# The opening of a fused FNet and GEGLU kernel: another order on four engines

## The chip, the cores and the metric

The kernel runs on one core of a Trainium2 chip. Times are device microseconds of that core. The core has a matrix engine (TensorE, PE in the profile), a vector engine (VectorE, DVE), an activation engine (ScalarE, ACT), a general engine (GpSimd, POOL), a queue engine for transfers (SyncE, SP) and sixteen transfer engines. Each engine takes its own instructions in order. Where one engine needs what another makes, it waits on a semaphore.

## The reference

The input `x` has 8 blocks of 3008 rows and 256 columns. It is Fourier-transformed along its rows and along its columns, and the real part goes through a gated feed-forward block:

```python
X = np.fft.fft(x, axis=1)
X = np.fft.fft(X, axis=2)
y = X.real.reshape(24064, 256)
g = y @ w_gate                       # 256 x 1536
gelu = 0.5 * g * (1.0 + erf(g / sqrt(2)))
out = (gelu * (y @ w_val)) @ w_out   # 1536 x 256
```

## The kernel before

**The transform.** A row index is written as 94 groups of 32. The kernel folds each block first: rows and their mirror rows (the same rows counted from the end) are added, and columns are folded in the same way, which leaves an even and an odd half (`eo`, lines 221 to 229). The forward rows come with plain transfers; the mirror rows come with an indirect transfer (`gather`, line 163) over a small table of indices that POOL makes (`index_consts`, lines 270 to 273). Then a matrix G of sines and cosines is applied along the rows (`s1`, line 513, called stage 1 here). Its result is copied out of PSUM into the tile A (line 519 on ACT, line 521 on DVE). For block 0 the matrix II (identities, one of them negated) joins and transposes the pieces of A (`ch`, line 535; copies into Z at 541 and 543). The matrix TP of twiddle factors completes the rows (`tp_e`, lines 591 and 596; copies into the tiles E and O at 601 and 603). The transform along the columns isn't applied to the data; it is multiplied into the weights: `make_w` (lines 451 to 470) makes the weights for E, for O, and for O negated (`minus`: W_sb or w_minus, lines 466 to 470) from `w_raw` and the matrix CW.

**The feed-forward part.** Each block is cut into three chunks of at most 512 columns, and each chunk into 12 slices of the 1536. For a slice, `l1_gate` takes a PSUM tile `ps_g`, multiplies the even half E into it and adds the odd half O (line 674 for each matmul); ACT applies Gelu (line 690). `l1_value` does the same in a tile `ps_v`. `l1_gate2` and `l1_value2` reuse the two tiles for the mirrored columns, with the negated weights. The products land in `h_sb` (lines 713, 730, 738), and `l2_piece` (line 763) multiplies them with `w_out`. There are two PSUM buffers for `ps_g`, three for `ps_v`, two for `ps_dft` and one for `ps_o`; a tile that is taken when all buffers of its tag have been used takes the oldest of them, and its first write waits for that buffer's last reader.

**The order.** The program is written out by hand, with no scheduler: every engine gets its instructions in the order in which the Python code issues them. `opening()` brings block 0 to its first E and O; `feed()` then runs the 288 slices and threads the transforms of later blocks between them. What matters here is the order within `opening()`:

- SP issues the two transfers of the staged forward rows. POOL makes columns and rows of counting numbers (`pool_consts`, lines 276 to 279), the index table, and issues the first gather; then `pool_consts2` (lines 282 to 284) and the other transfers: a second gather, the remaining rows of block 0, the weights, block 1.
- DVE makes small columns from them (`vec_consts`, lines 316 to 321), fills constants (lines 296 to 313), and reduces the phases of G (`g_phases`, lines 331 to 346). Line 344 is the absolute value of the reduced phase, |d|; line 345 subtracts a quarter. ACT takes the sines of these for G (`g_rows`, line 351; `g_ends`, lines 357 and 361) and for CW (lines 366 to 376). DVE makes II (`identities`, lines 390 and 392) and finishes CW (`cw_rest`, lines 381 to 386).
- PE multiplies zeros meanwhile: 16 warm matmuls, and 8 more after the first two stage-1 groups (`warm`, line 832).
- DVE folds block 0 in five pieces: rows 9 to 12, 13 to 16, 5 to 8, 0, and 1 to 4. Each `fold_piece` is followed by its two stage-1 groups, `s1(0, jg, 0)` and `s1(0, jg, 1)`, for jg = 2, 1, 3, 0, called (jg, g) below. All copies of A but the last are on ACT.
- Between these lie the twiddle phases (`t_columns` line 397, `t_phases` lines 401 and 404, `t_reduced` lines 265 and 266, `t_sin` line 411, `t_write` line 415) and the load of the Gelu table (line 426).

Of the kernel before, what the change touches and what calls it, by code (L numbers as in the profile page):

```python
# [9 lines left out]
FP32 = mybir.dt.float32  # L10
BF16 = mybir.dt.bfloat16
AF = mybir.ActivationFunctionType
ALU = mybir.AluOpType
# [15 lines left out]
def kernel(  # L29
# [55 lines left out]
    def work(shape, dt, tag, bufs, name):  # L85
        return work_pool.tile(shape, dt, tag=tag, bufs=bufs, name=name)
# [167 lines left out]
    rr = work([128, 2 * NGP], FP32, "O", 2, "rr")  # L254
    rd = work([128, 2 * NGP + NK], FP32, "Z", 1, "rd")
    cf, cr, cd = (work([128, C], FP32, t, 4, f"small_{i}") for i, t in enumerate(("v", "v", "v")))
    tf, tr, td = (work([128, 128], FP32, t, 3, f"small_t{i}") for i, t in enumerate(("ve", "ve", "ve")))
    w_raw = work([128, 2, 2, F], BF16, "h", 2, "w_raw")

# [55 lines left out]
    def vec_consts():  # L315
        nc.vector.tensor_scalar(col_a, col_p, 0.5, -0.25, op0=ALU.mult, op1=ALU.add)
        nc.vector.tensor_scalar(col_a, col_a, MAGIC, -MAGIC, op0=ALU.add, op1=ALU.add)
        nc.vector.scalar_tensor_tensor(col_h, col_a, -2.0, col_p, op0=ALU.mult, op1=ALU.add)
        nc.vector.tensor_scalar(col_n0, col_p, 1.0 / C, None, op0=ALU.mult)
        nc.vector.tensor_scalar(sc_g[:, 1:2], col_h, -TWO_PI, None, op0=ALU.mult)  # L320
        nc.vector.tensor_scalar(sc_g[:, 0:1], col_h, TWO_PI, -TWO_PI, op0=ALU.mult, op1=ALU.add)

    def vec_consts2():
        nc.vector.tensor_scalar(col_e, col_h, -1.0, 1.0, op0=ALU.mult, op1=ALU.add)
        nc.vector.tensor_scalar(keep2, col_p, 1.0, -2.0, op0=ALU.min, op1=ALU.mult)


    def g_phases():
# [12 lines left out]
        d0, d1 = (_sub(rd, [[1, n]], o, part_num=NP) for o, n in ((2 * NGP, NK), (NGP, NGP)))  # L341
        nc.vector.scalar_tensor_tensor(d1, r[:, NK:], MAGIC, f[:, NK:], op0=ALU.subtract, op1=ALU.subtract)
        c = _sub(rd, [[1, NGP]], 0, part_num=NP)
        nc.vector.scalar_tensor_tensor(c, d1, -1.0, d1, op0=ALU.mult, op1=ALU.max)
        nc.vector.tensor_scalar(c, c, -0.25, None, op0=ALU.add)
        nc.vector.scalar_tensor_tensor(d0, r[:, 0:NK], MAGIC, f[:, 0:NK], op0=ALU.subtract, op1=ALU.subtract)

    def g_rows(j0, nj):

# [15 lines left out]
    def cw_phases():  # L365
        nc.scalar.activation(cf[:, 0:128], row_c, AF.Copy, scale=col_n0)
# [20 lines left out]

    def identities():

        nc.vector.tensor_scalar(  # L390
            _sub(II, [[128, 3], [1, 128]], 0), _sub(row_c, [[0, 3], [1, 128]], 0), col_p, None, op0=ALU.is_equal)
        nc.vector.tensor_scalar(II[:, 1, 1, :], row_c, col_p, -1.0, op0=ALU.is_equal, op1=ALU.mult)

    def t_columns():
        ps = psum("v")
# [274 lines left out]
    def ffn_work(b):  # L670
# [5 lines left out]
        def cols_of(ci, fc):  # L676
# [3 lines left out]
                cstate[ci] = {"h": h_tile(), "ps": {}, "pso": {}}  # L680
            return n, c0, E, O, cstate[ci], slice(fc * 128, (fc + 1) * 128)

        def l1_gate(ci, fc):
            def run():
                n, _, E, O, st, fs = cols_of(ci, fc)
                pg = psum("g")
                mm(pg, n, "g", "E", fs, E, True, False)
                mm(pg, n, "g", "O", fs, O, False, True)
                gl = gelu_tile()
                nc.scalar.activation(gl[:, 0, :n], pg[:, :n], AF.Gelu)  # L690
                st["ps"][fc] = [pg, gl]
            return run
# [12 lines left out]
        def l1_value(ci, fc):  # L705
            def run():
                n, c0, E, O, st, fs = cols_of(ci, fc)
                pv = psum("v")
                if three(ci, fc):
                    gl = st["ps"][fc][1]  # L710
                    mm(pv, n, "v", "E", fs, E, True, False)
# [4 lines left out]
                mm(pv, n, "v", "E", fs, E, True, True)  # L716
# [82 lines left out]
    def opening():  # L799
        stage[0] = stage_tile()  # L800
        xb[0] = xb_tile(0)
        for j0, nj, at in ((9, 8, 0), (0, 1, 8)):
            nc.sync.dma_start(
                out=_sub(stage[0], [[1, nj * C]], at * C),
                in_=ap_replace(x, ap=[[32 * C, NPX], [1, nj * C]], offset=x.offset + j0 * C))
        pool_consts()
        index_consts(0)
        cast_mirror(0, 9, 8)
        pool_consts2()
        cast_mirror(0, 5, 4)  # L810
        cast_forward(0, 1, 8)
# [23 lines left out]
            for f in fold_ops(0, j0, nj, nc.vector):  # L835
                f()

        vec_consts()
        vec_fills()
        warm(16)  # L840
        cw_phases()
        g_phases()
        columns = t_columns()
        g_rows(9, 7)
        cw_reduced()
        vec_fills2()
        vec_consts2()
        identities()
        cw_magnitude()
        cw_sin()  # L850
        cw_rest()
        g_ends()
        g_rows(1, 8)
        t_phases(columns)
        fold_piece(9, 4)
        first, second = fold_ops(0, 13, 4, nc.vector)
        first()
        t_reduced()
        second()
        s1(0, 2, 0)()  # L860
        s1(0, 2, 1)()
        t_sin()
        gelu_table()
        warm(8)
        fold_piece(5, 4)
        s1(0, 1, 0)()
        s1(0, 1, 1)()
        fold_piece(0, 1)
        s1(0, 3, 0)()
        s1(0, 3, 1)()  # L870
        fold_piece(1, 4)
        s1(0, 0, 0)()
        s1(0, 0, 1, "V")()
        minus = []
        make_w(0, 0, 256, m_at=minus, tag="o")()
        ch(0, 0, qs=(0,))()
        t_write()
        ch(0, 0, "V", qs=(1,))()
        ch(0, 1, qs=(0,))()
        ch(0, 1, "V", qs=(1,))()  # L880
        make_w(1, 0, 256, m_at=minus, m_engine="V", tag="g")()
        tp_e(0, 0, 0, "A", tag="v")()
        tp_e(0, 0, 1, "V", tag="v")()
# [155 lines left out]
```

## Time and profile before

| | us |
|---|---|
| median of 4 runs | 621.14 (619.97 to 621.4) |
| profiled execution | 621.0 |
| its span | 619.2 |
| PE busy in the span | 606.6 |
| VectorE busy | 576.5 |
| ScalarE busy | 425.3 |
| GpSimd busy | 508.8 |
| first gather issued / fold begins | 1.89 / 8.82 |
| first feed-forward matmul starts | 18.41 |

The span is the time between the first and the last instruction of one profiled execution. The profile lists busy times by engine, groups of instructions by source line, waits with what ended them, and the chain of work that ended last, which is followed backwards from the last instruction to whatever released it. A busy engine isn't the bound by itself; a wait counts where it lies on that chain. Starts are counted from the start of the span. An instruction's length runs from its start to its end, and on one engine the next can start some 0.1 us before that end.

### The profile page before, as it was taken

Reading aid. Unit: us, or ns where it says so; the run is one execution under the profiler, and the core shown is the slowest. Engines: PE = TensorE matmul, PEld = TensorE weight load, DVE = VectorE, ACT = ScalarE, POOL = GpSimd, SP = SyncE. Lnnn points to the kernel's source line nnn. Section 1 sums busy time; section 2 is a strip of 40 time slices with the busy share of each in tenths; the row PEclk is TensorE's granted clock in tenths of the full one; section 3 lists DMA queues with packets and bytes.
Section 4 is the critical chain, followed back from the end, with each engine's and each line's share of the span. In section 5 each row is a group of like instructions: output and inputs, shape, how many; then the busy total and the mean of one; then the engine's idle time right before and its main releaser. Section 6 shows DMA issues by size and latency. Waiting matters only on the chain.

```text
span 619.2 us, 12746 instructions
## 1 busy us (share of the span) xinstructions
PE 606.6 (98%) x4182; PEld 406.4 (66%) x4230; DVE 576.5 (93%) x940; ACT 425.3 (69%) x825; POOL 508.8 (82%) x513
## 2 busy tenths in 40 slices
PE   7999999999999999999999999999999999999997
PEld 4456666666666666666666666666666666666666
DVE  7789999999999999999999999999999999999992
ACT  6787677777766676666767677666776667666651
POOL 8979899999997999879997899969987555555561
PEclk8999999999999999999999999999999999999999
DMA  9951825546362354632653344543123322221123
GB/s 179 202 128 37 246 53 154 136 121 178 91 168 79 96 150 109 157 98 51 162 141 99 108 96 120 141 107 95 43 69 77 97 56 51 64 50 43 40 52 82
DMA packets 52466, 65.40 MB, mean 106 GB/s; under 512 B 7629, under 2 KB 47278, under 8 KB 50004
## 3 DMA queue, kind: packets, MB, share of 16 engines
q1 hardware_dynamic: 45472, 49.03, 30.3%
q0 software_dynamic: 6608, 15.29, 11.5%
q8 instruction: 33, 0.54, 0.4%
q10 hardware_dynamic: 320, 0.26, 0.2%
q14 instruction: 33, 0.27, 0.1%
HBM read 39.65 MB, written 30.17 MB: 113 GB/s over the span
## 4 chain that ended last, share of the span: by engine, by line
PE 93%; DMA 2%; issue 1%; SPq 1%; ACT 1%; DVE 1%; POOL 0%; DVEq 0%; POOLq 0%; ACTq 0%
PE ps_o L763 39%; PE ps_g L674 29%; PE ps_v L674 20%; PE ps_dft L555 2%; PE ps_dft L591 2%; DMA xb<-in_x_dram,idx 1%; SPq L668 1%; DMA out_dram<-out_sb 1%; PE ps_dft L451 1%; PE ps_o L832 0%; DMA O_sb<-yrow 0%; ACT A_sb L519 0%; PE ps_dft L535 0%; DVE h_sb L730 0%; ACT gelu_sb L690 0%
## 5 line engine op out<-in xcount | busy, mean ns | idle before, releaser
L738 POOL TENSOR_TENSOR h_sb<-gelu_sb,v_sb 128x512 bf16<-128x512 bf16 (+1 forms) x280 | 319.8, 1147 | 91.1 <-DVE v_sb L736 79.5
L763 PE MATMUL ps_o<-Wo_sb,h_sb 128*128 128x256 bf16 (+1 forms) x2232 | 334.5, 273 | 0.0
L763 PEld LDWEIGHTS <-h_sb 128*128 128x128 bf16 (+1 forms) x2304 | 228.7, 100 | 111.1 <-POOL h_sb L738 1.2
L690 ACT ACTIVATE gelu_sb<-ps_g 128x512 bf16<-128x512 f32 (+1 forms) x288 | 169.5, 589 | 99.5 <-PE ps_g L674 76.2
L718 DVE SCALAR_TENSOR_TENSOR ve_sb<-EB_sb,yw,ps_v 128x512 f32<-128x512 bf16 (+1 forms) x280 | 206.2, 737 | 20.8 <-PE ps_v L674 18.1
L674 PEld LDWEIGHTS <-W_sb 128*128 128x128 bf16 x1440 | 138.1, 98 | 81.6 <-issue 4.0
L734 DVE TENSOR_TENSOR h_sb<-gelu_sb,ps_v 128x512 bf16<-128x512 bf16 (+1 forms) x280 | 189.9, 678 | 1.4 <-ACT gelu_sb L699 1.0
L736 DVE SCALAR_TENSOR_TENSOR v_sb<-ve_sb,ps_v 128x512 f32<-128x512 f32 (+1 forms) x280 | 187.4, 669 | 0.0
L699 ACT ACTIVATE gelu_sb<-ps_g 128x512 bf16<-128x512 f32 (+1 forms) x288 | 168.8, 586 | 0.0
L674 PE MATMUL ps_g<-O_sb,W_sb 128*128 128x512 bf16 (+1 forms) x530 | 159.0, 374 | 2.8 <-DMA O_sb<-yrow 0.3
L674 PE MATMUL ps_g<-E_sb,W_sb 128*128 128x512 bf16 (+1 forms) x288 | 108.0, 375 | 0.7 <-ACT gelu_sb L699 0.3
L674 PE MATMUL ps_v<-E_sb,W_sb 128*128 128x512 bf16 (+1 forms) x287 | 107.6, 375 | 0.8 <-DVE W_sb L459 0.6
L674 PE MATMUL ps_v<-O_sb,W_sb 128*128 128x512 bf16 (+1 forms) x288 | 108.0, 375 | 0.1
L783 ACT ACTIVATE out_sb<-ps_o 128x512 f32<-128x512 f32 x92 | 55.0, 598 | 34.3 <-PE ps_o L763 34.1
L229 POOL TENSOR_TENSOR eo_sb<-ab_sb 94x512 bf16<-94x512 f32 (+1 forms) x70 | 77.7, 1112 | 0.4
L558 ACT ACTIVATE S_sb<-ps_dft 96x512 bf16<-96x512 f32 x56 | 33.0, 589 | 18.6 <-PE ps_dft L555 18.6
L225 POOL TENSOR_TENSOR ab_sb<-x_raw,x_raw 94x508 f32<-94x508 f32 (+1 forms) x30 | 33.0, 1100 | 0.0
L222 POOL TENSOR_TENSOR ab_sb<-x_raw,x_raw 94x508 f32<-94x508 f32 (+1 forms) x30 | 32.9, 1098 | 0.0
L555 PE MATMUL ps_dft<-eo_sb,G 94*96 94x256 bf16 x119 | 22.3, 272 | 0.0
L601 ACT ACTIVATE E_sb<-ps_dft 128x512 bf16<-128x512 f32 (+1 forms) x23 | 13.5, 588 | 8.9 <-PE ps_dft L591 8.9
L163 POOL DMA_INDIRECT x_raw<-in_x_dram,idx x18 | 17.2, 957 | 2.8 <-issue 0.6
L601 ACT ACTIVATE O_sb<-ps_dft 128x512 bf16<-128x512 f32 (+1 forms) x22 | 13.0, 589 | 7.6 <-PE ps_dft L591 7.0
(151 smaller groups left out, 206.2 us busy)
## 6 DMA issues: line engine op xcount, KB each, us to landing
out_dram<-out_sb SPq DMA_DIRECT2D x364, 64.0 KB
x_raw<-in_x_dram SPq DMA_DIRECT2D x10, 768.0 KB
Z_sb<-z SPq DMA_DIRECT2D x7, 768.0 KB
z<-S_sb SPq DMA_DIRECT2D x7, 576.0 KB
EB_sb<-yrow SPq DMA_DIRECT2D x6, 376.2 KB
z<-S_sb SPq DMA_DIRECT2D x7, 192.0 KB
x_raw<-in_x_dram SPq DMA_DIRECT2D x2, 640.0 KB
x_stage<-in_x_dram SPq DMA_DIRECT2D x1, 768.0 KB
```

The lines of the kernel that those rows point to most:

```text
L225: eng.tensor_tensor(ab(1, 1, up), mir(1, up), fwd(255, down), op=ALU.add)
L229: eng.tensor_tensor(_sub(eo, [[C, nj], [1, 128]], j0 * C + g * 128), ab(0, 0, [[1, 128]]), ab(1, 0, [[1, 128]]), op=op)
L555: nc.tensor.matmul(ps[:96, q * C : (q + 1) * C], G[:, j, :], _sub(eo, [[1, C]], j * C), start=(j == js[0]), stop=(j == js[-1]))
L674: nc.tensor.matmul(ps[:, :n], W[nm, part][:, fs], src, start=start, stop=stop, **kw)
L690: nc.scalar.activation(gl[:, 0, :n], pg[:, :n], AF.Gelu)
L699: nc.scalar.activation(_sub(gl, [[-1, n]], TOK + n - 1), pg[:, :n], AF.Gelu)
L718: nc.vector.scalar_tensor_tensor(ve[:, :n], EB_bufs[b][:, c0 : c0 + n], yw[:, fc : fc + 1], pv[:, :n], op0=ALU.mult, op1=ALU.add)
L734: nc.vector.tensor_tensor(st["h"][:, fc, 0, :n], gl[:, 0, :n], pv[:, :n], op=ALU.mult)
L736: nc.vector.scalar_tensor_tensor(_sub(vv, [[-1, n]], n - 1), ve[:, :n], 2.0, pv[:, :n], op0=ALU.mult, op1=ALU.subtract)
L738: nc.gpsimd.tensor_tensor(st["h"][:, fc, 1, :n], gl[:, 1, :n], vv[:, :n], op=ALU.mult)
L763: nc.tensor.matmul(pso[:m, half], st["h"][:, fc, sign, h0 : h0 + m], Wo_sb[:, fc, :], start=(fc == 0 and not (first and sign)), stop=(fc = ...
L783: nc.scalar.activation(_sub(osb, [[1, 2 * C]], 0, part_num=m), pso[:m, :], AF.Copy)
```

## The change

All of it is in the opening and in the first three feed-forward matmuls.

- POOL makes the index table and issues the first gather ahead of `pool_consts`.
- |d| and the identities move from DVE to ACT, the identities as Abs(column - row), then Relu(1 - that), then a negated copy. They use a new small tile, `apart`.
- `vec_consts` moves to the place where DVE would wait for |d|; its column `col_n0` stays early, in `vec_n0`. `cw_reduced` is issued before `g_rows`, and `t_phases` before `g_ends` and the second `g_rows`.
- `t_reduced` and `t_sin` come between the first two folds instead of inside the second.
- The eight warm matmuls become six, and one more is issued after (3, 1).
- The copy of (3, 1) into A goes from ACT to DVE. The copies of Z change engines: the first half of each pair on DVE, the second on ACT. `t_write` comes before all of `ch`.
- Before the first slice, the even halves of gate 0, value 0 and gate 1 are issued (`even_ahead`); `l1_gate` and `l1_value` take the tiles up from there. For the later slices nothing is changed.

```diff
@@ g_phases
-        nc.vector.scalar_tensor_tensor(c, d1, -1.0, d1, op0=ALU.mult, op1=ALU.max)
+        nc.scalar.activation(c, d1, AF.Abs)
+        nc.vector.scalar_tensor_tensor(d0, r[:, 0:NK], MAGIC, f[:, 0:NK], op0=ALU.subtract, op1=ALU.subtract)
+        vec_consts()
         nc.vector.tensor_scalar(c, c, -0.25, None, op0=ALU.add)
-        nc.vector.scalar_tensor_tensor(d0, r[:, 0:NK], MAGIC, f[:, 0:NK], op0=ALU.subtract, op1=ALU.subtract)
@@ identities
-        nc.vector.tensor_scalar(
-            _sub(II, [[128, 3], [1, 128]], 0), _sub(row_c, [[0, 3], [1, 128]], 0), col_p, None, op0=ALU.is_equal)
-        nc.vector.tensor_scalar(II[:, 1, 1, :], row_c, col_p, -1.0, op0=ALU.is_equal, op1=ALU.mult)
+        nc.scalar.activation(apart[:, 0:128], row_c, AF.Abs, scale=-1.0, bias=col_p)
+        nc.scalar.activation(
+            _sub(II, [[128, 3], [1, 128]], 0), _sub(apart, [[0, 3], [1, 128]], 0), AF.Relu, scale=-1.0, bias=1.0)
+        nc.scalar.activation(II[:, 1, 1, :], II[:, 0, 0, :], AF.Copy, scale=-1.0)
@@ ffn_work
+        ahead = {}
+
+        def even_ahead(nm, ci, fc):
+
+            n, _, E, _, _, fs = cols_of(ci, fc)
+            ps = ahead[nm, b, ci, fc] = psum(nm)
+            mm(ps, n, nm, "E", fs, E, True, False)
+
+        if b == 0:
+            even_ahead("g", 0, 0)
+            even_ahead("v", 0, 0)
+            even_ahead("g", 0, 1)
+
         def l1_gate(ci, fc):
...
-                pg = psum("g")
-                mm(pg, n, "g", "E", fs, E, True, False)
+                pg = ahead.pop(("g", b, ci, fc), None)
+                if pg is None:
+                    pg = psum("g")
+                    mm(pg, n, "g", "E", fs, E, True, False)
                 mm(pg, n, "g", "O", fs, O, False, True)
@@ opening
-        pool_consts()
         index_consts(0)
         cast_mirror(0, 9, 8)
+        pool_consts()
         pool_consts2()
...
-        vec_consts()
         vec_fills()
         warm(16)
+        vec_n0()
         cw_phases()
+        identities()
         g_phases()
         columns = t_columns()
+        cw_reduced()
         g_rows(9, 7)
-        cw_reduced()
         vec_fills2()
         vec_consts2()
-        identities()
         cw_magnitude()
         cw_sin()
         cw_rest()
+        t_phases(columns)
         g_ends()
         g_rows(1, 8)
-        t_phases(columns)
         fold_piece(9, 4)
-        first, second = fold_ops(0, 13, 4, nc.vector)
-        first()
         t_reduced()
-        second()
+        t_sin()
+        fold_piece(13, 4)
         s1(0, 2, 0)()
         s1(0, 2, 1)()
-        t_sin()
         gelu_table()
-        warm(8)
+        warm(6)
         fold_piece(5, 4)
         s1(0, 1, 0)()
         s1(0, 1, 1)()
         fold_piece(0, 1)
         s1(0, 3, 0)()
-        s1(0, 3, 1)()
+        s1(0, 3, 1, "V")()
+        warm(1)
         fold_piece(1, 4)
         s1(0, 0, 0)()
         s1(0, 0, 1, "V")()
         minus = []
         make_w(0, 0, 256, m_at=minus, tag="o")()
-        ch(0, 0, qs=(0,))()
         t_write()
-        ch(0, 0, "V", qs=(1,))()
-        ch(0, 1, qs=(0,))()
-        ch(0, 1, "V", qs=(1,))()
+        for pp in range(2):
+            ch(0, pp, "V", qs=(0,))()
+            ch(0, pp, qs=(1,))()
         make_w(1, 0, 256, m_at=minus, m_engine="V", tag="g")()
```

More of the change, by code (lines that the diff above doesn't have):

```diff
@@ L256 @@
     cf, cr, cd = (work([128, C], FP32, t, 4, f"small_{i}") for i, t in enumerate(("v", "v", "v")))
+    apart = work([128, C], FP32, "v", 4, "apart")
     tf, tr, td = (work([128, 128], FP32, t, 3, f"small_t{i}") for i, t in enumerate(("ve", "ve", "ve")))
@@ L318, in vec_consts @@
         nc.vector.scalar_tensor_tensor(col_h, col_a, -2.0, col_p, op0=ALU.mult, op1=ALU.add)
-        nc.vector.tensor_scalar(col_n0, col_p, 1.0 / C, None, op0=ALU.mult)
         nc.vector.tensor_scalar(sc_g[:, 1:2], col_h, -TWO_PI, None, op0=ALU.mult)
@@ L325, in vec_consts2, with vec_n0 @@
         nc.vector.tensor_scalar(keep2, col_p, 1.0, -2.0, op0=ALU.min, op1=ALU.mult)
+    def vec_n0():
+        nc.vector.tensor_scalar(col_n0, col_p, 1.0 / C, None, op0=ALU.mult)
     def g_phases():
@@ L707, in run @@
                 n, c0, E, O, st, fs = cols_of(ci, fc)
-                pv = psum("v")
+                pv = ahead.pop(("v", b, ci, fc), None)
+                if pv is None:
+                    pv = psum("v")
+                    mm(pv, n, "v", "E", fs, E, True, not three(ci, fc))
                 if three(ci, fc):
                     gl = st["ps"][fc][1]
-                    mm(pv, n, "v", "E", fs, E, True, False)
                     mm(pv, n, "v", "O", fs, O, False, True)
@@ L715, in run @@
                     return
-                mm(pv, n, "v", "E", fs, E, True, True)
                 ve = ve_tile()
```

## The prediction

> **What bounds the kernel now.** I read the whole-program views first. The chain of work that ended last gives its shares by engine:
>
> ```profile
> PE 93%; DMA 2%; issue 1%; SPq 1%; ACT 1%; DVE 1%; POOL 0%; DVEq 0%; POOLq 0%; ACTq 0%
> ```
>
> TensorE (PE) is the bound, and no line of its steady state is touched. The change can only move the moment at which the feed-forward matmuls start; what follows then shifts as one piece. So I followed the same chain through the opening, in order of time (start, length, what):
>
> ```profile
> 1.89 6.91 DMA xb<-in_x_dram,idx
> 8.80 0.02 issue
> 8.82 0.19 DVE eo_sb L221
> ...
> 10.59 2.73 PE ps_o L832 x8
> 13.32 0.33 PE ps_dft L513 x4
> 13.65 0.02 issue
> 13.68 2.03 ACT A_sb L519 x5
> 15.71 0.05 issue
> 15.76 0.39 PE ps_dft L535 x2
> ...
> 18.13 0.70 DVE O_sb L603
> ```
>
> The gather of the first mirror rows lands at 8.80, VectorE (DVE) folds, eight warm matmuls (L832) hold PE until 13.1, five copies of A on ScalarE (ACT) run one behind the other until 15.7, then the channel step (L535), the E and O copies and, at 18.87, the first gate's odd half. Next come the timelines of single engines, for what is beside the chain (start, length, engine, line; in brackets the idle time before):
>
> ```profile
> 5.80 1.04 ACT L351 ACTIVATE G<-rd,sc_g 94x336 bf16<-94x336 f32 x2 [2.06 <-DVE rd L345]
> 8.18 0.15 DVE L386 CAST CW<-col 128x1 bf16<-128x1 f32 x1
> 12.96 0.28 DVE L225 TENSOR_TENSOR eo_sb<-xb,x_stage 94x127 bf16<-94x127 bf16 x1
> 13.16 0.18 DVE L221 TENSOR_TENSOR eo_sb<-xb 94x8 bf16<-94x8 bf16 x1
> 14.16 0.57 PE L513 MATMUL ps_dft<-G,eo_sb 94*128 94x96 bf16 x5
> 15.11 0.56 DVE L521 CAST A_sb<-ps_v 128x384 bf16<-128x384 f32 x1 [1.11 <-PE ps_v L513]
> 18.73 0.48 DVE L470 TENSOR_SCALAR w_minus<-ps_g,keep 128x256 bf16<-128x256 f32 x1
> ```
>
> To be seen: DVE has finished its constants at 8.33, half a microsecond before the gather; it folds without a gap from 8.82 to 14.0, and then waits 1.11 for PE.
>
> **Gather first (POOL).** Four small instructions (L276 to L279, 0.84 to 1.37) go behind it, so it is issued near 1.37 instead of 1.89: 0.5 earlier. Does it land earlier? The DMA view of 2 to 5.4 us says what moved in that time (packets, MB, share of 16 engines):
>
> ```profile
> q1 hardware_dynamic: 161, 0.74, 80.6%
> q0 software_dynamic: 4, 0.02, 2.4%
> ```
>
> The staged forward rows (q1) hold the engines; the gather, issued 1.5 us before this ended, moved almost nothing. It waits for bandwidth. Gain between 0 and 0.5; I take 0, nearest to that row. POOL's total is unchanged, so the second gather stays at 3.9. What waits behind the gather's 1.13 of POOL time is late: row_k is ready at about 3.06 instead of 1.37, row_c still near 3.26.
>
> **G's constants.** The DVE chain of g_phases started at 2.64; it now waits for row_k and starts at about 3.11 (+0.47). L342 moves from 4.19 to 4.66 and ends at 5.23. |d| goes to ACT: 94x408 f32, nearest row L351 (94x384, 0.55 each), so 5.29 to 5.85; meanwhile DVE does L346 and vec_consts, five dependent small operations, 0.7 by their old rows, to 5.92. Then L345 (0.37) ends at 6.29: G's sines start at 6.32 instead of 5.80, +0.5. The identities add 0.40 + 0.55 + 0.29 on ACT (rows L366, L351, L372); they run from 3.6 to 4.8 in the 2.06 idle shown above: nothing on the path. If that cover were gone, they would cost 1.24. Here a rule speaks against the change: the Trainium skill, "ScalarE: Activation LUTs", Rules for kernel authors, sends relu and the like to VectorE, up to about three times faster per element in bf16. By the row, |d| on DVE took 0.58 for 408 f32 elements, so the move is even; by the rule it would be 0.19 against 0.55 and the move would cost 0.36 more. I take the row: the operands are f32.
>
> **When folding starts.** ACT's magnitude and two sines follow G's first rows, so cw_rest on DVE, which ended at 8.33, ends at about 8.33 + 0.52 = 8.85. DVE comes free just when the gather lands. Even a gather at 8.3 would gain nothing here, and the forward rows 1 to 8 of block 0 (cast_forward, issued 4.85, landed 6.9 later, 11.75) let fold_piece(5,4) start no earlier than the old 11.86. So the DVE folds keep their times: 0, at worst +0.1. t_reduced merely swaps with half a fold. Later on ACT, t_phases, the ends and G rows 1 to 8 finish at 10.7 (old 9.3), t_sin at 11.0, two A copies at 12.0, the Gelu table at 13.3 and its dump at 13.5 (old 13.25). That is still before it matters.
>
> **Warm matmuls.** 8 become 6 before (1,*), and one goes in later. Two at half clock are 0.43 each, so PE is free at about 12.25; the (1,0) matmuls, whose folds are ready at 12.4, start at 12.45 instead of 13.11. Then 0.33, 0.33, 0.40, 0.40 as before: (3,1) is issued at 13.57 and its result stands at 14.14.
>
> **The shared copy.** This is the step that decides. s1(0,3,1) is now copied by DVE, in program order ahead of fold_piece(1,4). DVE is free at 13.20 (old 13.16), waits for PE until 14.18, copies (0.47 to the next start) and folds only then: 14.65 to 15.49 instead of 13.16 to 14.0. Behind it wait the (0,*) matmuls: (0,0) at 15.20, (0,1) at 15.54, result 15.87, DVE copy 15.91 to 16.47. ACT has one copy less, but its last one now waits for the fold: 15.57 to 16.06. Before, both engines had finished A at 15.70. The channel step needs both, so its second matmul is at 16.5 and the step is about 0.65 late. Bounds: with PE at full clock (3,1) is done 0.4 earlier, giving +0.3; with a later fold start, +0.9. The halves of ch swap engines, with the same number of copies on each, 0.
>
> **Even halves ahead.** gE(0,0), vE(0,0), gE(0,1) now precede the first odd half. PE had two gaps there (0.46 from 18.41, less 0.22 work, and 0.05): room for two. But the third takes the second of two ps_g buffers, in which make_w's result still lies; its last reader is w_minus (L470), 18.73 to 19.21, on DVE behind the O copy. So gO(0,0) goes from 18.87 to 19.27 + 0.22 = 19.49; vO ends its slot at 19.92 instead of 19.52 (+0.40). gE(0,1), 0.22, is then done already: +0.2 net. Without that wait it would be -0.26.
>
> **Sum.** 0 (gather and folds) + 0.65 (A) + 0.2 (odd halves) = +0.85, rounded to +0.8. Against the profiled execution, span 619.2 and 621.0 with what lies around it, that gives 620.0 and 621.8. The median of the runs is 621.14, 0.14 above this execution, so 621.9. Downstream the chain waits only for PE, ACT and DVE work that shifts along (VectorE at 26, ACT at 33), so it is passed on whole.
>
> **Rivals.** *Faster:* the gather and the other loads come earlier, or (3,1) is done before DVE needs it. For it: DVE waited 0.49 for the gather, and ACT's five serial copies were on the chain. Its best: fold_piece(1,4) cannot start before its rows (issued 7.74, 5.3 to landing, 13.04), 0.12 earlier; DVE's last copy then ends at 15.0 instead of 15.70; with -0.26 from the even halves, -0.96: 620.2. Against it: (3,1) depends on the fold that ends at 13.24, so the round trip has to fit in nothing.
>
> *Slower, by the clock:* the wait on DVE leaves PE idle, and the clock falls. Two stretches (PE busy in the third column, clock behind POOL's):
>
> ```profile
> 8.00:11.40 3.40, 1.50 (x12) 0.77 (x13) 2.88 (x11) 3.02 (x9) 3.40 (x5) 0.96 1.09 191
> 11.40:14.80 3.40, 3.40 (x29) 2.29 (x28) 2.59 (x10) 2.92 (x6) 3.40 (x6) 0.53 1.31 176
> ```
>
> PE was busy for 1.50 of 3.40, with one pause of 2.1, and the clock was 0.53 in the next stretch. The skill's "TensorE: Matmul & The Clock Gate", Part 1, wants an idle window of about 3.4 us for that; by it, new pauses of 0.4 to 0.8 cost nothing. The row shows that a shorter pause was enough. In the changed kernel PE would be busy for about 2.6 of 3.4 between 11.4 and 14.8 (1.0 warm, 1.5 stage 1, 0.1 of the rest) and again between 14.8 and 18.2. If a stretch with less than some three quarters busy is punished, 3.4 us of matmuls run at half speed, up to 1.7, of which about 1.2 falls on PE's own chain: +2.0, 623.1. It decides from the point where PE's share in such a stretch drops under what the gate accepts, which lies between 1.50 and 3.04 of 3.40 by the rows.
>
> *Nothing:* ACT's saved copy and PE's early start cancel the DVE wait: within 0.3, 621.1.
>
> **How the numbers follow.** Main case 0.55 (own range +0.3 to +1.3, 621.4 to 622.4), faster 0.20 (620.2 to 621.0), clock 0.15 (622.4 to 623.8), nothing 0.10. A range from 620.4 to 623.0 leaves out about 2 in 10: the better half of the faster case and the worse half of the clock case. 0.2% is 1.24 us, about what a measurement of this kernel can tell from no change. Slower by more: the clock case, and a tenth from the main case's upper end, 0.25. Faster by more needs all bounds at once and something unseen: 0.09. The rest, 0.66, is within it.
>
> **What would show it.** Right: the gather issued near 1.4 and landing at 8.6 to 8.9; G's first sine near 6.3; a DVE idle of about 1 us before an A copy that stands ahead of the last fold; the first channel matmuls near 16.2 to 16.5; the third even half waiting for w_minus. Wrong: folds that start before 8.5, that copy without a wait, or a clock of 0.5 after 15.

## The result, and the profile after

| | before | after |
|---|---|---|
| median of the runs, us | 620.96 (54 runs, 619.5 to 622.85) | 621.96 (33 runs, 620.74 to 624.57) |
| ratio to before | 1 | 1.0018 [1.0011, 1.0025] |
| profiled execution / its span, us | 621.0 / 619.2 | 622.56 / 620.7 |

The changed kernel is about 1.1 us slower (0.0018 of 620.96; the interval gives 0.7 to 1.55). The chain of work that ended last has the same bound as before, TensorE:

```profile
PE 91%; DMA 1%; SPq 1%; issue 1%; DVE 1%; ACT 1%; POOL 0%; DVEq 0%; POOLq 0%; ACTq 0%
```

The timelines of single engines in the changed kernel (start, length, engine, line; in brackets the idle time before, and who ended it). First the constants:

```profile
1.66 1.11 POOL L163 DMA_INDIRECT xb<-in_x_dram,idx  x1 [0.62 <-POOL idx L272]
3.36 0.58 DVE L334 SCALAR_TENSOR_TENSOR ff<-row_j,row_k 94x408 f32<-94x408 f32 x1 [0.23 <-POOL row_k L280]
6.42 1.04 ACT L355 ACTIVATE G<-rd,sc_g 94x336 bf16<-94x336 f32 x2 [0.52 <-DVE rd L350]
8.80 0.16 DVE L390 CAST CW<-col 128x1 bf16<-128x1 f32 x1
8.88 0.19 DVE L221 TENSOR_TENSOR eo_sb<-x_stage,xb 94x8 bf16<-94x8 f32 x1
```

The phases of G wait for row_k, G's sines start at 6.42 (5.80 before), and DVE's last constant and its first fold follow each other without a gap at 8.88 (8.82 before). Then stage 1. First the kernel before, its last fold on DVE and its last copy of A on ACT:

```profile
13.58 0.42 DVE L225 TENSOR_TENSOR eo_sb<-xb 94x508 bf16<-94x508 bf16 x1
15.18 0.52 ACT L519 ACTIVATE A_sb<-ps_g 128x384 bf16<-128x384 f32 x1
```

The changed kernel, on DVE:

```profile
13.04 0.28 DVE L225 TENSOR_TENSOR eo_sb<-xb,x_stage 94x127 bf16<-94x127 bf16 x1
13.71 0.56 DVE L526 CAST A_sb<-ps_dft 128x384 bf16<-128x384 f32 x1 [0.39 <-PE ps_dft L518]
...
14.61 0.41 DVE L225 TENSOR_TENSOR eo_sb<-xb 94x508 bf16<-94x508 bf16 x1
15.46 0.56 DVE L526 CAST A_sb<-ps_v 128x384 bf16<-128x384 f32 x1 [0.44 <-PE ps_v L518]
```

DVE finishes a fold, waits 0.39 for the result of (3, 1), copies it, and only then begins the last fold, which ends at 15.02 (14.0 before). A is complete at 16.02 (15.70 before). Last, the first feed-forward matmuls: one line of before (PE, the odd half of gate 1), then the changed kernel on DVE and PE:

```profile
20.61 0.59 PE L674 MATMUL ps_g<-O_sb,W_sb 128*128 128x512 bf16 x2
```

```profile
19.63 0.69 DVE L608 CAST O_sb<-ps_v 128x512 bf16<-128x512 f32 x1 [1.76 <-PE ps_v L601]
20.24 0.47 DVE L475 TENSOR_SCALAR w_minus<-ps_g,keep 128x256 bf16<-128x256 f32 x1
20.77 0.39 PE L679 MATMUL ps_g<-E_sb,W_sb 128*128 128x512 bf16 x1 [0.54 <-DVE w_minus L475]
21.00 0.38 PE L679 MATMUL ps_g<-O_sb,W_sb 128*128 128x512 bf16 x1
22.30 0.59 PE L679 MATMUL ps_g<-O_sb,W_sb 128*128 128x512 bf16 x2
```

The third even half waits 0.54 for w_minus, with the first odd half behind it. The odd half of gate 1 starts at 22.30 (20.61 before).

So the two profiles differ by +1.69 at gate 1, in three pieces: A complete, +0.32; from there to the copy of O, 3.61 instead of 2.43, +1.18; from that copy to gate 1's odd half, 2.67 instead of 2.48, +0.19. In the middle piece only the copies of Z and `t_write` have moved. They don't explain it: without a half-clock stretch there, the piece takes 2.27 to 2.45 in the experiments below that have the new order (e1, e3, e7 to e11), and 2.43 in the kernels with the old one (before, e4, e6, e12). The stretches of the changed kernel explain it (window, its length, PE busy, PEld, DVE, ACT, POOL, granted PE clock, DMA share, GB/s):

```profile
7.40:11.40 4.00, 2.05 (x19) 1.34 (x19) 3.16 (x13) 3.87 (x15) 3.72 (x5) 1.00 1.04 187
11.40:15.50 4.10, 2.62 (x33) 1.49 (x32) 3.25 (x12) 3.44 (x8) 3.80 (x7) 0.99 1.32 185
15.50:19.10 3.60, 3.60 (x24) 2.65 (x21) 1.75 (x5) 1.85 (x5) 2.99 (x4) 0.53 1.21 192
```

Both profiled executions have one stretch at half clock. Before, it lay between 11.4 and 14.8, in stage 1; after, it lies in the channel step. In these two single executions it hides part of the edit's cost in stage 1 and puts another on the channel step. To tell edits from clock, each run's mean granted clock was used beside its time. A stretch of 3.5 us at 0.53 takes 1.65 us of 620 and so lowers the mean to about 0.997; more than one such stretch lowers it to 0.994 or less. The number of stretches in a run is worked out from its mean in this way; no profile shows more than one. In the table, every experiment stands beside the runs of before on its own chip:

| median us (number of runs) | all runs | clock 0.998 or more | 0.995 to 0.997 | 0.994 or less |
|---|---|---|---|---|
| after | 621.96 | 620.90 (3) | 621.62 (22) | 622.89 (10) |
| *before, with the next four* | 620.79 | 620.14 (18) | 620.98 (32) | 622.03 (1) |
| e1: copy on ACT | 621.02 | 620.90 (2) | 621.02 (10) | 621.90 (2) |
| e2: two halves ahead | 621.94 | 620.50 (2) | 621.93 (10) | 622.80 (2) |
| e3: more warm matmuls | 622.14 | 621.13 (6) | 622.21 (15) | 623.05 (1) |
| e4: front alone | 621.27 | 620.81 (5) | 621.35 (8) | |
| *before, with the next four* | 620.39 | 619.70 (19) | 620.58 (44) | 622.39 (2) |
| e5: copy alone | 621.99 | 620.62 (2) | 622.00 (12) | |
| e6: two halves alone | 620.00 | 619.50 (12) | 620.46 (10) | |
| e7: early warm matmuls | 621.66 | 621.55 (18) | 623.37 (2) | |
| e8: copy behind the fold | 619.74 | 619.70 (21) | 621.89 (1) | |
| *before, with the next four* | 620.53 | 620.16 (17) | 620.83 (31) | |
| e9: e8 with the old front | 619.75 | 619.75 (20) | | |
| e10: gather second | 621.62 | 620.75 (2) | 621.65 (11) | |
| e11: e8 without early warm | 620.16 | 619.54 (3) | 620.07 (6) | 621.25 (4) |
| e12: early warm alone | 620.88 | 620.88 (13) | | |

Runs of the kernel before with one stretch are 0.67 to 0.88 us slower than those with none (620.98 - 620.14, 620.58 - 619.70, 620.83 - 620.16). The runs of before that the result was measured against have no clock on record, so the changed kernel is set beside all three chips: inside the class of one stretch it is slower by 0.6 to 1.0. It has more than one stretch in 10 of 35 runs, against 3 of 164 of the kernel before, and none in 3 of 35, against 54 of 164.

A class says how many stretches a run had, not where. In the profiles the place matters: in the channel step a stretch costs 1.2 to 1.4 (3.61 in after and 3.83 in e5, for 2.43), in stage 1 about 0.5 (from the start of folding to A 6.88 in before, for 6.34 and 6.38 without a stretch in e6 and e12). Nor does a class hold everything else equal: how early the rows land may go with it, and no run here separates the two.

### The profile page after: what moved, and what is told of

The parts are those of the page before. It is cut to its first block, busy times and chain, and to the rows that moved or that the text cites. A ratio compares the mean times of both kernels' runs of the same rounds, so it can differ in the third digit from the quotient of the medians.

```text
span 620.7 us, 12746 instructions
## 1 busy us (share of the span) xinstructions
PE 606.8 (98%) x4181; PEld 406.3 (65%) x4229; DVE 576.0 (93%) x938; ACT 426.3 (69%) x828; POOL 508.0 (82%) x513
## 4 chain that ended last, share of the span: by engine, by line
PE 91%; DMA 1%; SPq 1%; issue 1%; DVE 1%; ACT 1%; POOL 0%; DVEq 0%; POOLq 0%; ACTq 0%
PE ps_o L784 38%; PE ps_g L679 29%; PE ps_v L679 19%; PE ps_dft L560 2%; PE ps_dft L596 2%; SPq L673 1%; DMA out_dram<-out_sb 1%; PE ps_dft L456 1%; DMA O_sb<-yrow 0%; ACT gelu_sb L710 0%; DVE h_sb L751 0%; PE ps_dft L540 0%; DVE v_sb L757 0%; DVE W_sb L464 0%; POOL h_sb L759 0%
```

## The experiments

The theory: the shared copy costs most, since it waits for PE ahead of the last fold, and the third even half adds 0.2. The rivals: the clock is what costs; the new front (gather, constants) costs; or the edits cost nothing and a stretch at half clock only moved. Each experiment's ratio is to the runs of before on its chip. Four readings of each profile recur: when folding starts, when A is complete, when the copy of O starts, and when gate 1's odd half starts.

| us | fold starts | last fold ends | A complete | O copy | gate 1's odd half | half clock |
|---|---|---|---|---|---|---|
| before | 8.82 | 14.00 | 15.70 | 18.13 | 20.61 | stage 1 |
| after | 8.88 | 15.02 | 16.02 | 19.63 | 22.30 | channel step |
| e1 | 8.88 | 14.05 | 15.76 | 18.14 | 20.81 | stage 1 |
| e2 | 8.87 | 15.18 | 16.34 | 19.68 | 22.01 | channel step |
| e3 | 8.87 | 16.03 | 17.02 | 19.30 | 21.97 | stage 1 |
| e4 | 8.88 | 14.38 | 15.75 | 18.18 | 20.65 | stage 1 |
| e5 | 8.25 | 14.44 | 15.44 | 19.27 | 21.75 | channel step |
| e6 | 8.27 | 13.43 | 14.61 | 17.04 | 19.31 | none |
| e7 | 8.88 | 14.91 | 15.91 | 18.33 | 21.00 | none |
| e8 | 8.88 | 13.97 | 14.96 | 17.25 | 19.53 | none |
| e9 | 8.26 | 13.41 | 14.41 | 16.69 | 18.96 | none |
| e10 | 8.99 | 15.82 | 16.82 | 19.27 | 21.94 | stage 1 |
| e11 | 8.88 | 13.97 | 14.97 | 17.24 | 19.52 | none |
| e12 | 8.71 | 13.90 | 15.09 | 17.52 | 20.00 | none |

**e1, the copy back on ACT.** From the changed kernel:

```diff
-        s1(0, 3, 1, "V")()
+        s1(0, 3, 1)()
```

> The changed kernel with one thing undone: the copy of (3,1) into A is on ScalarE again, so the last fold no longer waits for it. Theory that the copy ahead of the fold is the main cost: the last fold ends near 14.2 instead of 15.0, ScalarE's five copies end near 15.3, the first channel matmul comes 0.5 to 0.7 earlier at the same clock, and the time falls by 0.65 us, to 621.3 (0.1%). Theory that the clock alone is the cost: the fold is earlier, but matmuls after 15 us still run at half speed and the time stays within 0.2 us of the changed kernel's 621.96. Theory that nothing but chance separates the kernels: 621.0 to 622.0 with no order.

Measured: 621.02, ratio 1.0005 [0.9997, 1.0013]. The DVE timeline of this kernel:

```profile
13.63 0.42 DVE L225 TENSOR_TENSOR eo_sb<-xb 94x508 bf16<-94x508 bf16 x1
14.86 0.56 DVE L526 CAST A_sb<-ps_v 128x384 bf16<-128x384 f32 x1 [0.82 <-PE ps_v L518]
18.14 0.69 DVE L608 CAST O_sb<-ps_v 128x512 bf16<-128x512 f32 x1 [1.04 <-PE ps_v L601]
```

The last fold ends at 14.05 again, and the copy of O starts where it did before (18.14 and 18.13). One word takes most of the loss away. What is left, 0.20 at gate 1, is the even halves. But the profile of e1 also has its stretch in stage 1, so e1 and after differ in the clock as well: part of their distance at gate 1 is that. In time, with one stretch in both, e1 is 0.6 faster than after (621.02 to 621.62).

**e5, the copy alone.** From the kernel before, one word:

```diff
-        s1(0, 3, 1)()
+        s1(0, 3, 1, "V")()
```

> The kernel before with one thing of the change: the copy of (3,1) into A is on VectorE, ahead of the last fold. Theory: VectorE waits for it, the last fold ends 1.0 to 1.5 later (near 15.3), the first channel matmul comes 0.5 to 0.9 later than 15.76 and the time rises by 0.5 to 0.9 us. Rival, that the copy itself is free and only TensorE's clock after 15 us costs: the first channel matmul comes within 0.2 of 15.76 wherever the clock is full.

Measured: 621.99, ratio 1.0028 [1.0016, 1.0040]: 1.6 slower, more than was expected and more than the whole change costs. Its DVE timeline:

```profile
8.25 0.19 DVE L221 TENSOR_TENSOR eo_sb<-x_stage,xb 94x8 bf16<-94x8 f32 x1
13.14 0.56 DVE L521 CAST A_sb<-ps_dft 128x384 bf16<-128x384 f32 x1 [0.39 <-PE ps_dft L513]
14.03 0.41 DVE L225 TENSOR_TENSOR eo_sb<-xb 94x508 bf16<-94x508 bf16 x1
14.88 0.56 DVE L521 CAST A_sb<-ps_v 128x384 bf16<-128x384 f32 x1 [0.44 <-PE ps_v L513]
```

It is the picture of the changed kernel, the 0.39 wait included, 0.6 earlier since folding started 0.6 earlier. From the start of folding to A: 7.19. Without the copy and at full clock the same distance is 6.34 (e6) and 6.38 (e12); with it, 7.03 (e7), 7.14 (after), 7.19 (e5). So the copy costs A 0.65 to 0.85 at full clock, some 0.75. Ahead of the fold stand 0.39 of wait and 0.48 of copy; a little of that comes back because ACT has one copy less behind it. With the stretch in stage 1 it is 7.83 (e10) against 6.88 (before): +0.95. The rest of the 1.6 is not the copy's own length: the stretch of e5 lies in the channel step, which takes 3.83 instead of 2.43. At full clock e5 is 0.92 slower than before (two runs), with one stretch 1.42.

**e8, the same copy behind the fold.** From the changed kernel; with it go seven early warm matmuls (e7), one warm matmul less, and two halves ahead instead of three:

```diff
-            even_ahead("g", 0, 1)
...
         g_rows(1, 8)
+        warm(7)
         fold_piece(9, 4)
...
-        s1(0, 3, 1, "V")()
-        warm(1)
         fold_piece(1, 4)
+        s1(0, 3, 1, "V")()
         s1(0, 0, 0)()
```

> The changed kernel with three edits: the copy of (3,1) stays on VectorE but stands behind the last fold, only two even halves go ahead, and seven warm matmuls fill TensorE's longest pause (the single one after (3,1) is left out). Theory: the last fold ends near 14.1, A is complete near 15.1 instead of 15.7, the first odd half of gate 1 comes 0.6 to 0.9 earlier than in the kernel before, and the time falls by 0.5 to 0.9 us against it, to about 620.2. Rival, that the waits return later in the opening or behind slice 30: the odd half is earlier, the time is that of the kernel before within 0.2 us.

Measured: 619.74 (22 runs, 619.36 to 621.89), ratio 0.9990 [0.9982, 0.9997], faster than both kernels. Its DVE timeline:

```profile
13.55 0.42 DVE L225 TENSOR_TENSOR eo_sb<-xb 94x508 bf16<-94x508 bf16 x1
13.88 0.55 DVE L526 CAST A_sb<-ps_dft 128x384 bf16<-128x384 f32 x1
14.40 0.56 DVE L526 CAST A_sb<-ps_v 128x384 bf16<-128x384 f32 x1
17.25 0.69 DVE L608 CAST O_sb<-ps_v 128x512 bf16<-128x512 f32 x1 [1.04 <-PE ps_v L601]
```

No bracket stands behind the two A copies: PE's results are there when DVE comes. From the start of folding to A it is 6.08 here, 6.09 in e11 and 6.15 in e9, some 0.25 less than without the shared copy. In the opening, sharing the copies is worth something; its place ahead of the fold cost three times that. In time this doesn't show by itself: at full clock e8 and before are level (619.70 both), though gate 1 is 1.08 earlier in the profile. The lower median goes with the clock: 21 of 22 runs without a stretch, against 19 of 65 of before on that chip.

**e2, two halves ahead instead of three.** From the changed kernel:

```diff
-            even_ahead("g", 0, 1)
```

> The changed kernel with only two even halves ahead (gate 0 and value 0); gate 1's even half goes back to its old place. Theory that the third one waits for w_minus and holds up the odd halves: gate 0's odd half starts within 0.1 of the end of the O copy, the odd half of gate 1 comes 0.45 to 0.5 earlier against the O copy, and the time falls by 0.45 us, to 621.5. Rival, that the wait is hidden further on by VectorE: the odd half of gate 1 is earlier, but the span is the same.

Measured: 621.94, ratio 1.0013 [1.0005, 1.0021]. From the O copy to gate 1's odd half it is 2.33 instead of 2.67, 0.34 less, where 0.45 to 0.5 was expected. The time, expected to fall by 0.45, doesn't separate from that of the changed kernel.

**e6, two halves ahead alone.** From the kernel before: `even_ahead` with

```diff
+            even_ahead("g", 0, 0)
+            even_ahead("v", 0, 0)
```

> The kernel before with the even halves of gate 0 and value 0 ahead of the first odd half, and not that of gate 1. Theory: value 0's even half fills the wait for the O copy, the odd half of gate 1 comes 0.2 earlier than 20.61, and the time falls by 0 to 0.25 us; three ahead showed plus 0.2 at the same place. Rival, that the order of these halves changes nothing: within 0.05 of 20.61.

Measured: 620.00, ratio 0.9995 [0.9989, 1.0002]. In the columns of equal clock it stands 0.2 (619.50 to 619.70) and 0.1 (620.46 to 620.58) under before. The lines of its profile, DVE's first fold, ACT's last copy of A, DVE's copy of O, and gate 1's odd half on PE:

```profile
8.27 0.19 DVE L221 TENSOR_TENSOR eo_sb<-x_stage,xb 94x8 bf16<-94x8 f32 x1
14.15 0.46 ACT L519 ACTIVATE A_sb<-ps_g 128x384 bf16<-128x384 f32 x1
17.04 0.69 DVE L603 CAST O_sb<-ps_v 128x512 bf16<-128x512 f32 x1 [0.86 <-PE ps_v L596]
19.31 0.59 PE L674 MATMUL ps_g<-O_sb,W_sb 128*128 128x512 bf16 x2
```

Over all profiles the distance from the O copy to gate 1's odd half is 2.67 with three halves ahead (after, e1, e3, e7, e10), 2.47 to 2.48 with none (before, e4, e5, e12), and 2.27 to 2.33 with two (e2, e6, e8, e9, e11). The third half turns a gain of about 0.2 into a loss of 0.2.

**e4, the front alone.** The kernel before with the new order up to the first fold:

```diff
-        pool_consts()
         index_consts(0)
         cast_mirror(0, 9, 8)
+        pool_consts()
...
-        nc.vector.scalar_tensor_tensor(c, d1, -1.0, d1, op0=ALU.mult, op1=ALU.max)
+        nc.scalar.activation(c, d1, AF.Abs)
```

and with the identities, `vec_consts`, `cw_reduced` and `t_phases` where the changed kernel has them; `t_reduced` and `t_sin` stay where they were.

> The kernel before with only the front of the change: gather first, |d| and identities on ScalarE, vec_consts moved, cw_reduced and t_phases reordered. Everything from the first fold on is as before. Theory: the fold starts between 8.8 and 8.95 as before (8.82), and the time is that of the kernel before within 0.2 us. Rival, that the earlier gather is worth something: the fold starts near 8.4 and the time falls by 0.3 to 0.5. Rival, that the later constants of G cost something: the fold starts after 9.0, plus 0.2 to 0.5.

Measured: 621.27, ratio 1.0003 [0.9995, 1.0012]: not told from before. Folding starts at 8.88, and the fold of rows 5 to 8 waits 0.32 for its rows, as the one line of its DVE timeline shows:

```profile
12.31 0.19 DVE L221 TENSOR_TENSOR eo_sb<-xb 94x8 bf16<-94x8 bf16 x1 [0.32 <-DMA xb<-in_x_dram]
```

**e10, the gather second again.** From the changed kernel:

```diff
+        pool_consts()
         index_consts(0)
         cast_mirror(0, 9, 8)
-        pool_consts()
```

> The changed kernel with one thing undone: pool_consts comes ahead of the first gather again. Theory that the late row_k is what delays G's constants: g_phases starts near 2.2 to 2.6 instead of 3.36, cw_rest ends near 8.1 to 8.4 instead of 8.95, and the fold starts when the gather lands (8.2 to 8.9). The time falls by 0 to 0.4 us against the changed kernel. Rival, that |d| on ScalarE is what delays them: cw_rest still ends after 8.8 and nothing changes.

Measured: 621.62, ratio 1.0015 [1.0007, 1.0024]. DVE's timeline:

```profile
8.17 0.15 DVE L390 CAST CW<-col 128x1 bf16<-128x1 f32 x1
8.99 0.19 DVE L221 TENSOR_TENSOR eo_sb<-x_stage,xb 94x8 bf16<-94x8 f32 x1 [0.67 <-issue]
14.52 0.56 DVE L526 CAST A_sb<-ps_dft 128x384 bf16<-128x384 f32 x1 [1.20 <-PE ps_dft L518]
```

The constants are 0.63 earlier (8.17 for 8.80), so it was the late row_k that had held them. The fold still starts only at 8.99, after 0.67 of idle time. The profile names no releaser for it; the constants being done, the gathered rows are what is left to wait for. The last line is the case that the prediction drew: the stretch lies in stage 1, the wait is 1.20, and A is complete at 16.82.

**e3, eight and three warm matmuls instead of six and one.**

```diff
-        warm(6)
+        warm(8)
...
-        warm(1)
+        warm(3)
```

> The changed kernel with four more warm matmuls in the two pauses of TensorE: eight instead of six after the first two stage-1 groups, three instead of one after (3,1). Theory that these pauses let the clock fall: no stretch at half clock between 15 and 19 us in the profile, and the time falls by 0.5 to 0.9 us against the changed kernel. Rival, that the copy and the third even half are the whole loss: the time stays within 0.2 us, or rises by up to 0.4 where the added matmuls run at half clock and hold up stage 1.

Measured: 622.14, ratio 1.0020 [1.0013, 1.0027]. The clock fell all the same, while the warm matmuls ran (PE's timeline; the window's columns as above):

```profile
10.59 3.28 PE L853 MATMUL ps_o<-gelu_sb 128*128 128x512 bf16 x8
```

```profile
10.60:14.00 3.40, 3.40 (x18) 1.40 (x16) 2.69 (x10) 3.23 (x7) 3.40 (x6) 0.59 1.28 187
```

Eight warm matmuls at half clock hold PE until 13.87, and stage 1 behind them: A at 17.02. Over the runs they did one thing: more than one stretch is seen in 1 of 22, where the changed kernel has 10 of 35. It gained nothing in time. The other experiments point the same way. Without early warm matmuls, the kernels with six in this place have more than one stretch in 18 of 89 runs (after 10 of 35, e1 2 of 14, e2 2 of 14, e10 0 of 13, e11 4 of 13); those with eight have it in 4 of 235 (before 3 of 164, e3 1 of 22, and e4, e5 and e6 none of 49).

**e7, warm matmuls earlier.** From the changed kernel, seven more in PE's order ahead of the first stage-1 group, where PE paused:

```diff
         g_rows(1, 8)
+        warm(7)
         fold_piece(9, 4)
```

> The changed kernel with seven more warm matmuls in TensorE's longest pause, before the first stage-1 group (8.0 to 9.7). Theory that the clock is part of the loss: no stretch at half clock between 10 and 20 us; gate 1's odd half comes 0.5 to 0.7 later than the kernel before has it (20.61), instead of 1.7 later, and the time falls to about 621.5. Rival, that the half clock comes whatever is done there: it shows in 10 to 20 us again and the time stays near 622.

Measured: 621.66, ratio 1.0019 [1.0011, 1.0027]. A stretch of its profile, then DVE's timeline:

```profile
14.80:18.20 3.40, 3.34 (x36) 2.42 (x34) 1.90 (x6) 3.01 (x8) 2.63 (x4) 1.00 1.15 180
```

```profile
13.61 0.56 DVE L526 CAST A_sb<-ps_dft 128x384 bf16<-128x384 f32 x1 [0.39 <-PE ps_dft L518]
14.50 0.41 DVE L225 TENSOR_TENSOR eo_sb<-xb 94x508 bf16<-94x508 bf16 x1
```

The clock is full, the channel step takes 2.42 again, and the wait of 0.39 and the late fold are still there: they don't come from the clock. At gate 1 e7 is only 0.39 behind before, but its median is nearly as slow as that of after. Against before at equal clock it is 1.85 slower (621.55 to 619.70). Its opening accounts for 1.0 of that: gate 1 at 21.00, where e12, the kernel before with the same early warm matmuls, has 20.00. In its profile 1.0 more is lost between 143 and 176 us, where PE waits 0.7 for a late transfer (O_sb<-yrow).

**e12, the early warm matmuls alone**, in the kernel before (the same line).

> The kernel before with seven warm matmuls in TensorE's longest pause and nothing else. Theory: no stretch at half clock in 10 to 20 us, ScalarE's copies of A start 0.3 to 0.5 earlier against the fold, and the time falls by 0.3 to 0.6 us. Rival, that the half clock in stage 1 is hidden by ScalarE's copies: within 0.15 us of the kernel before. Rival, that the added matmuls hold up the first stage-1 group: plus 0.2 to 0.6.

Measured: 620.88, ratio 1.0005 [0.9997, 1.0013]. A fall of 0.3 to 0.6 was expected, and a rise of 0.35 came. All 13 runs have the full clock, and over e7, e8, e9 and e12 it is 72 of 75, where before has 54 of 164. So the early warm matmuls do keep the clock up. Yet at full clock e12 is 0.72 slower than before (620.88 to 620.16): what the clock gave is lost again, after the opening. The profile of e12 ends 0.19 behind before, though gate 1 was 0.61 ahead; between 143 and 226 us, where it falls back, its list of waits has on PE (source, then sum, number and longest):

```profile
PE ps_g L674 <- DMA O_sb<-yrow: 0.9, 1, 0.9
```

**e11, e8 without the early warm matmuls** (the line `warm(7)` taken out).

> The best version so far (copy of (3,1) behind the last fold, two even halves ahead) without the seven early warm matmuls. Theory that they hold the clock: in part of the executions a stretch of 3.4 us at half clock returns between 10 and 19 us, the executions spread more widely, and the median is 0.3 to 0.6 us above 619.74. Rival, that the order of the copies is the whole gain: the median is within 0.15 us of 619.74.

Measured: 620.16 (13 runs), ratio 0.9994 [0.9986, 1.0003]. Its profile goes through the opening as e8's does (gate 1 at 19.52 and 19.53), and then its lead of 1.08 over before is lost within 10 us, near 80 us (same list):

```profile
PE ps_dft L632 <- DMA Z_sb<-z: 1.0, 1, 1.0
```

Four of its 13 runs had more than one stretch at half clock; e8 had none such in 22. By the clock that favours e8; but at full clock e11 is 0.62 under before (three runs), where e8 is level, and the two intervals overlap.

**e9, e8 with the front of before**: gather second, |d| and identities on DVE, the constants, `t_reduced` and `t_sin` in their old order.

```diff
+        pool_consts()
         index_consts(0)
         cast_mirror(0, 9, 8)
-        pool_consts()
...
-        nc.scalar.activation(c, d1, AF.Abs)
+        nc.vector.scalar_tensor_tensor(c, d1, -1.0, d1, op0=ALU.mult, op1=ALU.max)
```

> The kernel before (gather, constants and identities in their old places) with the rest of the best version: seven warm matmuls before the first stage-1 group and six after it, the copy of (3,1) on VectorE behind the last fold, two even halves ahead, the new order of the channel step's copies. Theory that the new front makes the fold wait for constants instead of the gather: here the fold starts at 8.2 where the gather is early, or when it lands, and the time is 0.2 to 0.5 us below that of the same version with the new front (619.74). Rival, that later rows bind the folds anyway: the time is within 0.15 us of it.

Measured: 619.75 (20 runs, 619.15 to 620.35), ratio 0.9987 [0.9981, 0.9994]. From DVE's timeline:

```profile
8.26 0.19 DVE L221 TENSOR_TENSOR eo_sb<-x_stage,xb 94x8 bf16<-94x8 f32 x1
13.85 0.56 DVE L521 CAST A_sb<-ps_v 128x384 bf16<-128x384 f32 x1
```

Folding starts 0.62 before e8's, and gate 1's odd half is 0.57 earlier. The two medians are equal (619.75 and 619.74), but they come from two chips, on which before itself differs. Beside its own before at full clock e9 is 0.41 faster (619.75 to 620.16), and e8 is level; over all runs the ratios are 0.9987 and 0.9990, with intervals that overlap. So the new front may cost up to 0.6 by the profiles and 0.4 by the times, and these runs don't settle it. e8 and e9 both beat the kernel before.

## Why the prediction was right, and where it wasn't

The prediction was 621.9; 621.96 was measured, inside the range and in the class that it held likeliest. The main step was right, but the sum had errors that cancelled, a rival was partly true, and that the two figures lie 0.06 apart is luck. The prediction added 0.8 to 621.14, the median of four runs; over 54 runs before is 620.96, and the loss is 1.0 to 1.1.

- **Gather first.** Right that there is no gain. It was issued at 1.66, not 1.37, since the wait for the index table is 0.62 when nothing lies between; it took 6.9 and landed at 8.56. The transfers of 2 to 5.4 us fit the reason given (packets, MB, share of 16 engines): the forward rows moved nearly all of it, the gather next to nothing.

```profile
q1 hardware_dynamic: 189, 0.77, 83.5%
q0 software_dynamic: 9, 0.04, 8.4%
```

- **G's constants.** Right: sines at 6.42 for 6.32. |d| took 0.54 on ACT for 0.58 on DVE: the trace's row held, and the factor of about three that the Trainium skill ("ScalarE: Activation LUTs", Rules for kernel authors) gives to VectorE, stated there for bf16, did not carry over to these f32 operands.
- **When folding starts.** Right between the two profiles (8.88 for 8.82, predicted 8.85), but wrong as a bound. It took the 8.82 of one execution as the time at which the rows land. With the old front, e5, e6 and e9 fold from 8.25 to 8.27, and e6 starts rows 5 to 8 at 11.36, which the step held impossible before 11.86. Landing times scatter by 0.7 from profile to profile (8.16 to 8.86 with the new front); the old constants were ready at 8.33 and could use an early gather, the new ones, ready at 8.96, can't. "0, at worst +0.1" should have been 0 to +0.6 in a profile; in the times it is not settled (e9).
- **Warm matmuls and the shared copy.** Mechanism right: the wait, the late fold and the late A are in every profile that has the copy there, and go when it goes behind the fold (e8, e11). Size: +0.65 predicted; some +0.75 at full clock, +0.95 with the half-clock stretch in stage 1. The profile of after shows only +0.32 because it had the full clock in stage 1 and before had not: it compares two clocks. The lower bound of the step (+0.3, "with PE at full clock") made the same mistake: it sped PE up after the change, and left before at half clock.
- **Even halves ahead.** Right: +0.19 for +0.2, and for two halves -0.15 to -0.2, where -0.26 was said for the case without the wait. The wait for w_minus stands in the line.
- **The rival by the clock.** It was listed as another outcome; in fact it came beside the main one. In the profile the stretch moved to the channel step and cost 1.18 there, as the rival's 1.2 said, while the 0.5 that it had cost before in stage 1 went away. Over the runs, before has such a stretch in most of its executions too. What is new is that 10 of 35 have more than one, and only 3 have none. Those ten raise the median from 621.62, that of the 22 with one stretch, to 621.96: +0.3. The rival blamed the wait on DVE. The counts point elsewhere, to the warm matmuls that were taken out: 18 of 89 runs with six, 4 of 235 with eight. e5, which has the wait and all eight, has none of 14; e3, which differs from after in warm matmuls alone, has 1 of 22. The prediction counted their removal as a gain for PE only. This is a count and not a trace of those runs, e3 adds two further ones behind (3, 1), and e10 with six has none of 13: it is likely, not shown.
- **Sum.** Between the two profiles the 1.69 splits into fold start +0.06, copy at full clock +0.78 (7.14 for 6.36, the middle of e6 and e12), the stretch in the channel step instead of stage 1 +1.18 - 0.52, and odd halves +0.19. Over the runs it closes less exactly: copy and halves make +0.94 to +0.97 at full clock, where +0.8 was predicted from +0.65 and +0.2; measured are 0.6 to 1.0 with one stretch, and about 1.1 with the clock's share. Where the stretch lay in those runs is not known.
- **Passed on whole.** Nearly true between these two profiles: the first Gelu of slice 1 starts 1.70 later on ACT, the last Gelu of the program 1.55 later. It isn't a rule. In every profile the distance to before stays constant from slice 1 to about 70 us; then it shifts by up to 1.3 where a later block's rows or its Z come late (the lines of e11 and e12, and 0.3 in before itself near 93 us). Gains in the opening are partly given back there; e12, e11 and e7 show it.

## What to carry to other kernels

On an engine that works in order, a copy that waits for a round trip through another engine belongs behind the work that others wait for: in the opening, the same shared copy cost some 0.75 us ahead of the last fold, and saved 0.25 behind it. An early half of a product is worth issuing only into a buffer that is already free. And before two profiles are subtracted, set the clock of each stretch side by side: the same edit showed +0.32 or +0.95 according to where the half-clock stretch fell. Runs on different chips are compared through the kernel before on each.

## What the hardware showed that was not expected

- The clock fell after PE pauses much shorter than the stretch itself. The prediction had cited "TensorE: Matmul & The Clock Gate", Part 1, of the Trainium skill for an idle window of about 3.4 us. In the changed kernel PE was busy for 2.62 of 4.10 us, with no pause over 0.85, and 3.6 us at 0.53 followed. So no such idle window was needed here. PE's busy share in the stretch before doesn't decide alone either: in the same kernel 2.05 of 4.00 was followed by 0.99, and in e6 1.66 of 3.50 by full clock. What does is open.
- Whether an execution has the stretch varies from run to run with the same kernel: 54 of 164 runs of before have none. With seven warm matmuls in the first pause, 72 of 75 have none. What those kernels gain in clock is lost again later in e12 and e7 (0.7 and more at equal clock), and e8 loses 0.6 against e11 when each is set beside its own before at full clock (three runs of e11). The profiles of e12 and e7 show the same late transfer (0.9 and 0.7 of waiting for O_sb<-yrow between 143 and 176 us), that of e8 doesn't. Whether the warm matmuls cause it is not settled.
- The same gather, issued at 1.66, landed at 8.16 in the profile of e4, 8.56 in that of after and 8.86 in that of e1. With the old front folding started anywhere from 8.25 to 8.82. A single profile fixes the start of folding to no better than 0.6 us.
